# Attention and experts in one kernel: the main list turned four pauses later, weights split one call behind their load, the first expert product ordered behind the last attention sums

## The chip, the cores and the metric

The kernel runs on one core of one Trainium2 chip. A core has a matrix engine (TensorE, in the profile PE, with its weight loads as PEld), a vector engine (VectorE, DVE), an activation engine (ScalarE, ACT), a general engine (GpSimd, POOL), a queue engine that mostly issues transfers (SyncE, SP), and DMA engines that move data between memory and the core. Each engine takes its instructions in the order in which the program has them; semaphores make one wait for another. The metric is the device time of one execution in microseconds (us), lower is better. What can be told from no change in this study is about 0.3%.

## What is computed

The first half is linear attention for 8 batches, 8 heads, 576 tokens of 64 values, with features of exp(x) and exp(-x). The second half sends each of the 4608 tokens (512 values) through one of 8 experts, two products with a relu between them.

```python
def phi(x):
    proj = np.einsum('bhsd,df->bhsf', x, w_phi)
    proj = proj - np.max(np.abs(proj), axis=-1, keepdims=True)
    return np.concatenate([np.exp(proj), np.exp(-proj)], axis=-1)
q_p, k_p = (phi(q), phi(k))
kv = np.einsum('bhsf,bhsd->bhfd', k_p, v)
z = np.sum(k_p, axis=2)
num = np.einsum('bhsf,bhfd->bhsd', q_p, kv)
den = np.einsum('bhsf,bhf->bhs', q_p, z)[..., None] + 1e-06
x = num / den                      # to (B, S, 512)
...
fresh_e = int(np.argmax(logits[b, s]))
e = fresh_e if s == 0 or local_gate[b, s] < 0.5 else prev_e
...
h = np.maximum(x[b, s] @ w1[e], 0.0)
out[b, s] = p[e] * (h @ w2[e])
```

## The kernel before, in words

**Attention** runs in 72 steps over pairs of token chunks (`step`, L484). Its last sums are the matmuls of `num` (L404): they multiply the features of q with the summed kv, and DVE divides them (L421 to L424). In these steps the order on PE is the one in which the program is written; afterwards the planner orders PE too.

**The planner.** The program is written as tiles in pools and instructions that use them. A planner then reckons through the program and gives each engine its order: an instruction is issued when in its reckoning the inputs are there and a buffer of its pool is free, and the place in the code decides between instructions that are ready together. `issue_after(x)` puts what is written inside it behind instruction `x` on its engine; `high_priority` moves it up. A load or a split can therefore run far ahead of its place in the code.

**The experts** work on slots of up to four units of 128 tokens that share an expert. Two early slots (`eslots`, three units each) come from the first half of the batches and are worked while the list of all the rest is made; then come the slots of the main list (`moe`, L1196). The main list is planned by `plan_main` (L809): DVE counts, POOL gathers the list's rows into `lr` (L736), PE turns `lr` by two transposes (L753), DVE copies token numbers and probabilities (L755, L756). Then POOL can gather token rows `xg` (L984), and PE turns them (L1010).

**A slot** (`slots`, L1134) is `layer1` and `layer2`. `layer1` makes the hidden values in eight blocks of 128: a block is four groups of three matmuls (`three`, L1024 to L1026: high part by high part, low by high, high by low) into one of two PSUM banks (`psl`). Then ACT writes the relu's high part hh (L1063) and DVE the low part hl (L1064), after which the bank is free. For three units a block is 12 matmuls of 384 columns. `layer2` multiplies hh and hl with the second weights for each unit (again `three`), and DVE scales the result to y (L1122), which POOL scatters out (L1125).

**Pauses.** `layer1` calls a function from a list in the middle of each block and at its end, so a block has two pauses. For the two early slots these lists (`soon`, L158) hold the steps of planning: `go` and `rest` for the last gate in the first, `read` for the turn of the main list and `ahead` for its first gathers in the second. `read` is the next part of `plan_main`: L753 behind the last matmul written (`last_pe`), then L755 and L756. `later` holds the same for `layer2`: `listed` starts `plan_main` and its gathers.

**Weights.** A slot has eight slabs of 128 x 1024, four of each weight. `load` (L927) lets SP fetch a slab as `wraw` (512 KB, three buffers at this stage). `split` (L947) lets ACT cast it to a high part `whi` (L955) and DVE subtract to a low part `wlo` (L957). `spare` (L960) loads and splits one more slab if fewer are held than fit; `used` (L974) counts one slab as used and calls `spare`. `layer1` calls `used` after every second block, `layer2` calls `spare` or `used` after every second of its eight steps. The first early slot's slabs are loaded and split beside attention (`early_weights`, L472).

Of the kernel before, what the change touches and what calls it, by code (L numbers as in the profile page):

```python
# [55 lines left out]
class Kernel:  # L56
# [9 lines left out]
    def run(self):  # L66
        nc, tc, A = self.nc, self.tc, self.A
        act, dve = self.act, self.dve
        with ExitStack() as root:
            self.const = self.mkpool(root, "const", 1, "left")  # L70
            dram = self.mkpool(root, "dram", 1, "left", DRAM)
            self.xs = dram.tile([NT + 1, DM], F32, name="xs")


            self.lst = dram.tile([E * NT + 128, PLACE], F32, name="lst")
            first = self.const.tile([128, 256], F32, name="first")
            self.act.dma_start(first[:, 128:256], A["first"][:, 384:512])
            self.ident, self.w2 = first[:, 0:128], first[:, 128:256]
            self.cnt = self.const.tile([128, E], BF16, name="cnt")
            dve.memset(self.cnt, 0.0)  # L80

            warm = self.const.tile([128, E], BF16, name="warm")
            act.activation(warm, self.cnt, AF.Exp)

            self.wgi = self.const.tile([128, NHP, 2, 9], F32, name="wgi")
            self.pool.memset(self.wgi, 0.0)

            self.moe_early = self.mkpool(root, "moe_e", WE, "left")
            self.mxg = self.mkpool(root, "moe_xg", 2, "left")
            back, front = ExitStack(), ExitStack()  # L90
            self.back2 = self.mkpool(back, "back2", 2, "left")
            self.small = self.mkpool(back, "small", 1, "left")

            self.pr = self.small.tile([128, 2, NC, PLACE], F32, name="pr")
            self.pool.memset(self.pr, 0.0)
            self.pskv = self.mkpool(back, "pskv", 2, "left", PSUM)
            self.psb = self.mkpool(back, "psb", 2, "left", PSUM)


            self.front2 = self.mkpool(front, "front2", 2, "right")  # L100
            self.front3 = self.mkpool(front, "front3", 3, "right")
            self.feat = self.mkpool(front, "feat", 8, "right")
            self.psf = self.mkpool(front, "psf", 2, "right", PSUM)
            self.wphases = [(self.moe_early, WE)]

            self.scattering = False
            self.tail, self.eslots, self.scattered = False, [], []
            self.g, self.ch, self.kvb, self.lg, self.kvp, self.summed = {}, {}, {}, {}, {}, {}
            n = NBP * NHP * NC
            self.todo, self.turns, self.gates, self.background = [], [], [], []  # L110
            self.fetched = 0
            self.fetch_kq(0)
            self.fetch_kq(1)
            self.sp.dma_start(first[:, 0:128], A["first"][:, 256:384])
            self.fetch_v(0)
            self.fetch_v(1)
            self.fetch_kqv(2)
            self.consts()
            with tc.manual_schedule(engines={mybir.EngineType.PE}):
                for p in range(n // 2):  # L120
                    while self.fetched < n // 3 and self.fetched * 3 < 2 * p + 8:
                        self.fetch_kqv(self.fetched)
                    if p == FILL + 4:
                        self.background.append(self.table())
                    if FILL <= p < FILL + 4:
                        self.fill(p - FILL)
                    self.step(p, n)
            self.tail = True
            p = n // 2
            while p < n // 2 + KVLAG + 1 or self.todo or self.turns or self.gates:  # L130
                self.step(p, n)
                p += 1
            for x in self.background:
                for _ in x:
                    pass
            front.close()
            self.open_main(root)
            plan = self.plan_main()
            go = self.advance

            def rest():
                for _ in self.last_gate:
                    pass

            def listed():
                next(plan)
                next(plan)
                self.coming.append(self.by_size[4][0])

            def read():  # L150
                with tc.high_priority():
                    next(plan, None)
            no = lambda: None
            m = []

            def ahead():
                m.append(self.tokens(self.by_size[4][0], True))
            self.slots(self.eslots, soon=[[no, no, no, go, no, no, go, no, no, go, rest], [no, no, read, no, ahead]],  # L158
                       later=[[listed], [no, no] + [lambda k=k: m[0][k]() for k in range(4)]])
            back.close()  # L160
            self.open_rest(root)
            self.moe()
# [228 lines left out]
    def num(self, u, b, cs, kvs, bank=None):  # L391

        bp, hp = divmod(u, NHP)
        n, c0 = len(cs), cs[0]
        e = {}

        def mm(c, r, h, sg, kvs):
            i = u * NC + c
            q0 = i % 2 * 128
            if not e:  # L400
                t = bank or self.psb.tile([128, 512], F32, name="nm")
                e["t"] = t[:, 0:n * 2 * KV].rearrange("p (c k) -> p c k", c=n)
            k = slice(h * KV, h * KV + KV)
            self.pe.matmul(e["t"][r, c - c0, k], self.ch[i]["qp"][:, sg, h, q0 + r.start:q0 + r.stop],  # L404
                           kvs[:, sg, k], start=sg == 0, stop=sg == 1)


        for c in cs:
            k = [self.kvb[u] if c == 4 else kvs, kvs]
# [549 lines left out]

    def spare(self):  # L960

        while self.coming:
            s = self.coming[0]
            i = len(s.get("w", ()))
            if i == 8:
                self.coming.pop(0)
                continue
            if self.held < sum(n for _, n in self.wphases):
                self.load(s, i)
                self.split(s)  # L970
                self.held += 1
            return

    def used(self, n):  # L974
        for _ in range(n):
            self.held -= 1
            self.spare()
# [50 lines left out]
    def both(self, s, k, o, ah, al, c, first, last):  # L1028
# [6 lines left out]
        for z in (0, 1):  # L1035
            r = slice(64 * z, 64 * z + 64)
            self.last_pe = self.pe.matmul(o[r], ah.bitcast(F32)[:, r], w[z][:, c], start=first, stop=last)

    def hidden(self, n):
        return [self.mx2.tile([128, 8, n * 128], F32R, name=x, bufs=1) for x in ("hh", "hl")]  # L1040

    def layer1(self, s, between):

        act, dve = self.act, self.dve
        (xh, xl), w, n = s["x"], s["w"], s["n"]
        hh, hl = s["h"] = self.hidden(n)

        def pause():
            if between:
                between.pop(0)()  # L1050
        per = 2 if n == 2 else 1
        for f0 in range(0, 8, per):
            t = self.psl.tile([128, per, n * 128], F32, name="l1")
            for j in range(per):
                f = f0 + j
                wh, wl = w[f // 2]
                for d in range(4):
                    c = slice(d * 256 + f % 2 * 128, d * 256 + f % 2 * 128 + 128)
                    self.three(t[:, j, :], wh[:, c], wl[:, c], xh[:, d, :], xl[:, d, :], d == 0, d == 3)
                    if d % 2 and (d, j) != (3, per - 1):  # L1060
                        pause()
            hc = slice(f0, f0 + per)
            act.activation(hh[:, hc, :], t, AF.Relu)  # L1063
            dve.scalar_tensor_tensor(hl[:, hc, :], t, 0.0, hh[:, hc, :].bitcast(F32), ALU.max, ALU.subtract)  # L1064
            pause()
            if (f0 + per) % 2 == 0:
                self.used(1)
# [66 lines left out]
    def slots(self, order, held=None, soon=(), later=()):  # L1134
        first = order[0]
        if "x" not in first:
            for f in self.tokens(first):
                f()
        self.held = len(first.get("w", ()))
        self.coming = list(order)  # L1140
        for i, s in enumerate(order):
            while len(s.get("w", ())) < 8:
                self.spare()
            new = order[i + 1] if i + 1 < len(order) else None
            between = []
            for x in order[i + 1:i + 3 if new and len(new["ei"]) == 2 and s["n"] > 1 else i + 2]:
# [2 lines left out]
            if s["n"] > 1:  # L1149
                self.layer1(s, list(soon[i]) if i < len(soon) else [])  # L1150
                rest = between
            else:
                rest = self.layer1_one(s, between) + between
            if i < len(later):
                rest = list(later[i]) + rest
# [135 lines left out]
```

## Time and profile before

| | |
|---|---|
| times of three runs | 767.77, 768.43, 770.03 us (median 768.43) |
| the profiled execution | 768.59 us, of which the span is 766.8 us |
| attention's last sums (L404) | end near 299.6 us |
| first early slot, `layer1` and `layer2` | 299.5 to 337.7 us |
| second early slot, `layer1` begins | 337.74 us |
| the main list's gather issued by POOL (L736) | 336.87 to 338.37 us |
| main slabs 1, 2, 3, 4 issued by SP | 335.56, 337.64, 338.73, 341.98 us |

A timeline row has the start in us, the length in us, the engine, the line, the operation, the tile written and the tiles read, and in brackets the idle time in front of it and what ended it. A row of the waits has the waiting engine and line, what it waited for, the total in us, how many times, and the longest. A row of the windows has the stretch, its length, and busy time and count for PE, PEld, DVE, ACT and POOL, then the granted clock of PE, the share of DMA and GB/s. Matmuls overlap, so the step from one start to the next is what one costs, not its length.

### The profile page before, as it was taken

The numbers are of one execution on the slowest core, as the hardware profiler recorded it, in microseconds if no ns is written. First come the engines' busy times: TensorE is split into PE (matmuls) and PEld (weight loads), VectorE is DVE, ScalarE is ACT, GpSimd is POOL, SyncE is SP. The second block draws the span as 40 slices with busy tenths as digits, with TensorE's granted clock in tenths as the row PEclk, the third lists the DMA queues.
The fourth block names the chain that finished last, engine by engine and source line by source line (L and its number), as shares of the span: only waits on it lengthen the run. The fifth ranks groups of instructions, "written<-read, shape, count | busy, mean of one in ns | idle before, by whom it ended". The sixth has DMA issues, their size and how long they took to land. (4 is left out here: it accounts for less than half of the span.)

```text
span 766.8 us, 21974 instructions
## 1 busy us (share of the span) xinstructions
PE 739.7 (96%) x9319; PEld 637.3 (83%) x9319; DVE 451.0 (59%) x828; ACT 344.5 (45%) x648; POOL 181.9 (24%) x306
## 2 busy tenths in 40 slices
PE   7999999999998898989999999999999999999997
PEld 6999989989887887869888985789888768888885
DVE  5888888789878876665532347425323554544411
ACT  4776657666676664324421236314212453433300
POOL 0210103310374563433302041021202102101011
PEclk9999999999999999998999999999999999999999
DMA  6755545544766743248612799432398474432010
GB/s 201 240 169 140 152 127 141 152 130 138 227 179 182 217 118 107 86 149 275 205 52 69 287 366 324 146 124 82 124 352 284 142 242 165 138 123 97 1 38 29
DMA packets 66100, 125.04 MB, mean 163 GB/s; under 512 B 7220, under 2 KB 45300, under 8 KB 65950
## 3 DMA queue, kind: packets, MB, share of 16 engines
q1 hardware_dynamic: 57808, 101.03, 41.4%
q0 software_dynamic: 8016, 22.51, 8.2%
q8 instruction: 74, 1.21, 0.7%
q14 instruction: 26, 0.21, 0.1%
q10 hardware_dynamic: 176, 0.07, 0.0%
HBM read 102.05 MB, written 22.06 MB: 162 GB/s over the span
## 5 line engine op out<-in xcount | busy, mean ns | idle before, releaser
L955 ACT CAST whi<-wraw 128x1024 fp32r<-128x1024 f32 x88 | 92.2, 1048 | 134.5 <-PE l L1026 59.6
L957 DVE TENSOR_TENSOR wlo<-wraw,whi 128x1024 fp32r<-128x1024 f32 x80 | 97.8, 1223 | 88.7 <-ACT whi L955 88.6
L1024 PE MATMUL l<-xhi,whi 128*128 128x384 f32 (+2 forms) x352 | 127.1, 361 | 1.2 <-DVE g_es L617 0.6
L1026 PE MATMUL l<-xhi,wlo 128*128 128x384 f32 (+2 forms) x352 | 124.4, 353 | 0.0
L1025 PE MATMUL l<-xlo,whi 128*128 128x384 f32 (+2 forms) x352 | 124.3, 353 | 0.0
L1024 PE MATMUL l<-whi,hh 128*128 128x512 f32 x288 | 117.1, 407 | 0.0
L1025 PE MATMUL l<-wlo,hh 128*128 128x512 f32 x288 | 114.1, 396 | 0.0
L1026 PE MATMUL l<-whi,hl 128*128 128x512 f32 x288 | 113.6, 395 | 0.0
L285 ACT ACTIVATE kp<-sb 128x512 f32<-128x512 f32 x144 | 83.4, 625 | 58.5 <-DVE sb L281 55.5
L279 DVE TENSOR_REDUCE m<-pj 128x8 f32<-128x1024 f32 x72 | 87.7, 1218 | 35.0 <-PE pj L276 33.0
L1063 ACT ACTIVATE hh<-l 128x384 fp32r<-128x384 f32 (+1 forms) x84 | 44.9, 535 | 110.8 <-PE l L1026 110.8
L276 PE MATMUL pj<-first,kq 64*128 64x128 f32 x1152 | 85.8, 290 | 8.0 <-DMA kq<-in_kqT 4.2
L309 ACT ACTIVATE qp<-pj 128x512 f32<-128x512 f32 x144 | 79.6, 594 | 24.8 <-PE pj L294 12.9
L281 DVE TENSOR_TENSOR sb<-pj,m 128x1024 f32<-128x1024 f32 x72 | 88.1, 1223 | 3.5
L404 PE MATMUL nm<-kvs,qp 128*64 128x74 f32 x2304 | 88.4, 228 | 1.7 <-issue 0.9
L1064 DVE SCALAR_TENSOR_TENSOR hl<-l,hh 128x384 fp32r<-128x384 f32 (+1 forms) x84 | 51.4, 611 | 60.4 <-ACT hh L1063 60.3
L276 PEld LDWEIGHTS pj<-first,kq 64*128 64x128 f32 x1152 | 72.2, 192 | 15.1 <-issue 5.2
L404 PEld LDWEIGHTS nm<-kvs,qp 128*64 128x64 f32 x2304 | 80.6, 136 | 3.0 <-issue 1.5
L1024 PEld LDWEIGHTS l<-xhi,whi 128*128 128x128 f32 x352 | 66.8, 190 | 15.6 <-issue 5.6
L326 PE MATMUL kvp<-v,kp 128*64 128x65 f32 x2048 | 78.6, 226 | 1.0 <-issue 0.5
L1125 POOL DMA_INDIRECT out<-y,p_tokm x30 | 35.1, 1171 | 182.7 <-DVE y L1122 167.8
L326 PEld LDWEIGHTS kvp<-v,kp 128*64 128x64 f32 x2048 | 67.9, 139 | 5.6 <-ACT kp L285 1.2
(222 smaller groups left out, 926.1 us busy)
## 6 DMA issues: line engine op xcount, KB each, us to landing
wraw<-in_w1h SPq DMA_DIRECT2D x44, 512.0 KB
wraw<-in_w2h SPq DMA_DIRECT2D x44, 512.0 KB
kq<-in_kqT SPq DMA_DIRECT2D x47, 384.0 KB
v<-in_va SPq DMA_DIRECT2D x48, 195.0 KB
xs<-xo SPq DMA_DIRECT2D x48, 128.0 KB
whi<-in_w1h SPq DMA_DIRECT2D x8, 512.0 KB
wlo<-in_w1h SPq DMA_DIRECT2D x8, 512.0 KB
whi<-in_w2h SPq DMA_DIRECT2D x8, 512.0 KB
```

The source lines that it names most:

```text
L276: self.last_pe = self.pe.matmul(t[:, h, i % 2, j, :], kq[r, j, s], self.w2[r], start=True, stop=True)
L279: dve.tensor_reduce(m, f, AX.X, ALU.max, apply_absolute_value=True)
L281: self.last_dve = dve.tensor_sub(sb.rearrange("p h c j f -> p (h c j) f"), f, m.unsqueeze(2).broadcast_to([128, 8, 128]))
L285: self.last_act = act.activation(kp[:, :, :, sg, :].rearrange("p c h f -> p h c f"), sb[:, :, :, 0], AF.Exp, scale=1.0 - 2 * sg)
L309: self.act.activation(qp[:, sg].rearrange("p h (c r k) -> p (h c) r k", c=2, r=2), src, AF.Exp, scale=1.0 - 2 * sg)
L326: self.pe.matmul(t[r, sg, h], kp[:, h, sg, r], v[:, h], start=first and sg + h == 0, stop=last and sg + h == 2)
L404: self.pe.matmul(e["t"][r, c - c0, k], self.ch[i]["qp"][:, sg, h, q0 + r.start:q0 + r.stop], kvs[:, sg, k], start=sg == 0, stop=sg == 1)
L955: self.act.copy(hi, raw)
L957: (low or self.dve).tensor_sub(lo[:, c], raw[:, c], hi.bitcast(F32)[:, c])
L1024: mm(o, ah, bh, start=first, stop=False)
L1025: mm(o, ah, bl, start=False, stop=False)
L1026: self.last_pe = mm(o, al, bh, start=False, stop=last)
```

## The change

Three edits. `read` moves from the third entry of the second early slot's list to the seventh, and `ahead` from the fifth to the tenth. `spare` now first splits what the call before it loaded, then loads one slab and leaves its split to the next call; `asked` counts the loads of a slot in place of the finished splits, and a slot that begins splits whatever is still left. And the first matmuls of the first early slot's first product stand behind the last matmul of attention's sums on PE; `last_num` is used once and then empty.

```diff
-            self.slots(self.eslots, soon=[[no, no, no, go, no, no, go, no, no, go, rest], [no, no, read, no, ahead]],
+            self.slots(self.eslots, soon=[[no, no, no, go, no, no, go, no, no, go, rest], [no] * 6 + [read, no, no, ahead]],
...
-            self.pe.matmul(e["t"][r, c - c0, k], self.ch[i]["qp"][:, sg, h, q0 + r.start:q0 + r.stop],
+            self.last_num = self.pe.matmul(e["t"][r, c - c0, k], self.ch[i]["qp"][:, sg, h, q0 + r.start:q0 + r.stop],
...
     def spare(self):
+        self.landed()
         while self.coming:
             s = self.coming[0]
-            i = len(s.get("w", ()))
+            i = s.get("asked", len(s.get("w", ())))
             if i == 8:
                 self.coming.pop(0)
                 continue
             if self.held < sum(n for _, n in self.wphases):
                 self.load(s, i)
-                self.split(s)
+                s["asked"] = i + 1
+                self.loaded.append(s)
                 self.held += 1
             return
+
+    def landed(self, keep=0):
+        while len(self.loaded) > keep:
+            self.split(self.loaded.pop(0))
...
+    def behind(self):
+        x, self.last_num = self.last_num, None
+        return self.tc.issue_after(x.ins) if x else nullcontext()
...
-                    self.three(t[:, j, :], wh[:, c], wl[:, c], xh[:, d, :], xl[:, d, :], d == 0, d == 3)
+                    with self.behind():
+                        self.three(t[:, j, :], wh[:, c], wl[:, c], xh[:, d, :], xl[:, d, :], d == 0, d == 3)
...
-        self.held = len(first.get("w", ()))
-        self.coming = list(order)
+        self.held = first.get("asked", len(first.get("w", ())))
+        self.coming, self.loaded = list(order), getattr(self, "loaded", [])
         for i, s in enumerate(order):
-            while len(s.get("w", ())) < 8:
+            while s.get("asked", len(s.get("w", ()))) < 8:
                 self.spare()
+            self.landed()
```

## The prediction

> **What bounds the kernel now.** I read the page first, then the waits of TensorE, then the windows, then the timeline of each engine around the one wait that stands out.
>
> ```profile
> span 766.8 us, 21974 instructions
> PE 739.7 (96%) x9319; PEld 637.3 (83%) x9319; DVE 451.0 (59%) x828; ACT 344.5 (45%) x648; POOL 181.9 (24%) x306
> ```
>
> TensorE is busy for 96% of the span, so only its idle time and its clock can be won. Of its waits between 280 and 360 us, all at the seam from attention to the experts, one is large:
>
> ```profile
> PE pt L753 <- DMA lr<-lst,p_rim: 3.2, 1, 3.2
> PE l L1024 <- DVE g_es L617: 0.6, 1, 0.6
> PE l L1024 <- DVE hl L1064: 0.5, 1, 0.5
> ```
>
> The windows give PE, PEld, DVE, ACT, POOL, then the granted clock and the DMA. The clock falls to half late in 343.50:344.00 (0.92 is 16% of half a microsecond at half, so at 343.92) and is back at 350.75 (0.75: half of that stretch). After the seam PE is full: 400 to 420 stands for the later stages.
>
> ```profile
> 343.50:344.00 0.50, 0.00 (x0) 0.00 (x0) 0.00 (x0) 0.00 (x0) 0.40 (x1) 0.92 0.81 328
> 350.50:351.00 0.50, 0.50 (x3) 0.50 (x3) 0.00 (x0) 0.00 (x0) 0.50 (x1) 0.75 0.68 197
> 400.00:420.00 20.00, 20.00 (x94) 16.39 (x93) 4.96 (x7) 2.96 (x5) 4.91 (x5) 1.00 0.21 66
> ```
>
> So 3.2 us are idle and 6.8 us run at half clock: about 6.6 us at stake. The timeline of PE there:
>
> ```profile
> 337.74 0.33 PE L1024 MATMUL l<-xhi,whi 128*128 128x384 f32 x1
> ...
> 340.52 0.33 PE L1025 MATMUL l<-xlo,whi 128*128 128x384 f32 x1
> 340.69 0.34 PE L1026 MATMUL l<-xhi,wlo 128*128 128x384 f32 x1
> 344.23 0.42 PE L753 MATMUL pt<-first,lr 48*128 48x48 f32 x2 [3.20 <-DMA lr<-lst,p_rim]
> 344.58 0.69 PE L1024 MATMUL l<-xhi,whi 128*128 128x384 f32 x1
> ...
> 346.67 0.63 PE L1024 MATMUL l<-whi,hh 128*128 128x512 f32 x1
> 347.09 0.63 PE L1025 MATMUL l<-wlo,hh 128*128 128x512 f32 x1
> ...
> 348.37 0.52 PE L1024 MATMUL l<-xhi,whi 128*128 128x384 f32 x1
> ...
> 351.56 0.33 PE L1024 MATMUL l<-xhi,whi 128*128 128x384 f32 x1
> ```
>
> From 337.74 run block 0 of the second early slot (12 matmuls) and half of block 1 (6). Then the two transposes of the main list wait for their gather. Half a block, four matmuls of the second product and block 2 (348.37) follow; block 3 begins at 351.56. The question is whether block 2 really waited for L753. ACT and DVE answer:
>
> ```profile
> 339.64 1.05 ACT L955 CAST whi<-wraw 128x1024 fp32r<-128x1024 f32 x1 [3.44 <-DMA wraw<-in_w1h]
> 344.53 1.05 ACT L955 CAST whi<-wraw 128x1024 fp32r<-128x1024 f32 x1 [3.84 <-DMA wraw<-in_w1h]
> 345.49 0.48 ACT L1063 ACTIVATE hh<-l 128x384 fp32r<-128x384 f32 x1
> 345.87 1.04 ACT L955 CAST whi<-wraw 128x1024 fp32r<-128x1024 f32 x1
> ```
> ```profile
> 340.72 1.23 DVE L957 TENSOR_TENSOR wlo<-wraw,whi 128x1024 fp32r<-128x1024 f32 x1 [2.03 <-ACT whi L955]
> 341.87 0.74 DVE L1122 TENSOR_SCALAR y<-l,p_probe 128x512 f32<-128x512 f32 x1
> 345.61 1.23 DVE L957 TENSOR_TENSOR wlo<-wraw,whi 128x1024 fp32r<-128x1024 f32 x1 [3.00 <-ACT whi L955]
> 346.75 0.20 DVE L755 CAST p_tokm<-pt 128x48 int32<-128x48 f32 x1
> 346.87 0.20 DVE L756 COPY p_probm<-pt 128x48 f32<-128x48 f32 x1
> 346.99 0.55 DVE L1064 SCALAR_TENSOR_TENSOR hl<-l,hh 128x384 fp32r<-128x384 f32 x1
> ```
>
> Block 0 ended near 340.0, but its hh (L1063) stands on ACT behind the cast of the main list's second slab, which waits for its DMA until 344.53. There are two banks for the first product, so block 2 needs block 0's hl, done at 347.54. **Two waits lie side by side**, and removing the visible one uncovers the other.
>
> **The change part by part.** The sum is made against the profiled execution's own 768.59 us (span 766.8), 0.16 above the median of 768.43.
>
> **1. The main list four pauses on.** A block has two pauses, so `read` moves from the middle of block 1 to the middle of block 3, 24 matmuls later.
> - Block 1's other half follows at 0.173 a matmul (340.52 to 340.69) and ends at about 342.1. PE then waits for hh at 345.97: 3.9 idle in place of 3.2.
> - The four matmuls of the second product need only hh. At half clock they take 0.42 each (346.67 to 347.09), at full clock half of that. DVE's two copies go from in front of hl, which starts 0.24 earlier and ends at 347.30. Block 2 starts at 346.0 + 4 x 0.425 = 347.70 (cold) or 347.30 (warm), instead of 348.37: **-0.67 or -1.07**.
> - The transposes come back inside block 3 without a wait, 344.23 to 344.58: **+0.35**.
> - Clock: before, block 2 had 350.75 - 348.37 = 2.38 us at half clock, 1.19 lost. After, with the same instants, (350.75 - 347.70)/2 = 1.53: **+0.34**. If the clock falls one half of its 6.83 us later (347.33 to 354.17), block 2 starts warm: 3.43 - 1.19 = +2.24.
>
> Part 1 gives -0.67 + 0.35 + 0.34 = 0.0; with the late fall -1.07 + 0.35 + 2.24 = +1.5. A fall at 347.33 that ends at 350.75 gives -1.07 + 0.35 + 1.72 - 1.19 = -0.2.
>
> Behind the moved step stand two DVE copies and POOL's six gathers of token rows (before at 347.23 to 354.84). After, the copies run at about 352 and the gathers, 1.27 apart, are issued by about 361. Their first reader is at 367.81, so I cost this at nothing; were the rows later than that, each microsecond would be one of PE. SP's weight loads do not pass through `read`.
>
> ```profile
> 347.23 0.98 POOL L984 DMA_INDIRECT xg<-xs,p_tokm  x1 [3.33 <-DVE p_probm L756]
> 353.89 0.95 POOL L984 DMA_INDIRECT xg<-xs,p_tokm  x1 [0.30 <-PE l L1026]
> 367.81 0.60 PE L1010 MATMUL tr<-first,xg 128*128 128x128 f32 x4
> ```
>
> **2. Splits one call later.** Loads and splits keep their mutual order; only their place among the products moves. Does that move an instruction on ACT or DVE?
>
> ```profile
> 303.64 1.05 ACT L955 CAST whi<-wraw 128x1024 fp32r<-128x1024 f32 x1 [0.51 <-PE l L1025]
> 304.60 0.48 ACT L1063 ACTIVATE hh<-l 128x384 fp32r<-128x384 f32 x1
> ```
>
> This cast is written after block 5, yet runs ahead of block 1's hh: the planner issues what is ready, and the place in the code decides only between things ready together. The casts become ready by a freed buffer or a landed DMA. The new call also splits all that is left when a slot begins (`landed()` in `slots`), so the first three slabs of the main list are still written ahead of block 0's hh. **I take 0.** Bounds: the 1.1 of L1024's two short waits could go (-1.1); a slab late by one call costs up to 24 x 0.173 = 4.2, but slabs are ready long before use, as here by 24 us:
>
> ```profile
> 453.07 1.05 ACT L955 CAST whi<-wraw 128x1024 fp32r<-128x1024 f32 x1 [0.34 <-DMA wraw<-in_w1h]
> 477.27 0.50 PE L1024 MATMUL l<-xhi,whi 128*128 128x512 f32 x1
> ```
>
> **3. The first product behind the last sums.** One matmul now fills a hole:
>
> ```profile
> 295.06 0.44 PE L1024 MATMUL l<-xhi,whi 128*128 128x384 f32 x1
> 295.44 2.41 PEld L404 LDWEIGHTS nm<-kvs,qp 128*64 128x64 f32 x67 [0.19 <-ACT kvs L384]
> ```
>
> The sums wait 0.19 for ACT's copy of kvs, so without the matmul they would hardly start sooner. The matmul's 0.17 comes back behind them: **+0.17**, between -0.2 (they do start sooner) and +0.2. The products queue behind it; nothing but hh waits for them.
>
> Sum: 768.59 + 0.0 + 0 + 0.17 = **768.8**, with the other clock ends 768.5 to 770.3.
>
> **The rivals.**
> **A, the clock never falls.** PE is idle for 3.9 us, but with the four matmuls at full clock. Then -1.07 + 0.35 - 1.19 + 0.17 = -1.7: **766.9**. Against it: 3.2 idle were enough before. [...]
>
> **B, the order on ACT flips** (the planner puts block 0's hh ahead of the cast that waits). ACT is free at 340.69, hh ends at 341.1, DVE's y at 342.61, hl at 343.1: block 2 starts 5.27 earlier, no clock is lost: -5.27 - 1.19 + 0.35 + 0.17 = -5.9, **762.7**. If block 1's hh stays behind the cast, its hl ends at 347.3 and block 3 begins there instead of at 351.56: -4.26 + 0.35 + 0.17 = -3.7, **764.9**. For it: a landing half a microsecond later in the planner's reckoning is enough, and the splits have been lowered. Against it: nothing ahead of 341 that decides this order changes.
>
> **C, weights first (slower).** The third and fourth slabs, no longer held up, go ahead of block 0's hh and hl too. hh then comes at 347.6, hl after three more low parts (345.61 + 3 x 1.2 + 0.5) at 349.7: block 2 +1.33, transposes +0.35, part three +0.17, clock -0.66 or +1.05: **769.8 to 771.5**. It decides once hl ends after 348.37. For it: they are written ahead of hh. Against it: the third slab has that place already and still follows hh (345.87).
>
> **That part 2 reorders nothing** is my forecast, not a rival.
>
> **How the numbers follow.** Forecast 0.42 (768.5 to 770.3), A 0.12, B 0.30, C 0.16. The predicted time is 768.8. The range 762.5 to 770.6 takes in the forecast, A, B and C's lower part. About 0.3% (2.3 us) can be told from no change: faster is B and a little of A, 0.33; slower is C's upper half and the forecast's far end, 0.13; the same is 0.54.
>
> **What would show it.** Right: L753 without a wait, a wait of L1024 or of the second product's L1024 on ACT hh or DVE hl of 3 to 4 us from about 342, half clock behind it, ACT still cast, cast, hh. B: hh at about 340.6 and no gap over 2 us. C: two more casts before hh. I am wrong also if the second slab's DMA lands at another time than 344.5, or if PE has new idle after 360.

## The result, and the profile after

The changed kernel takes **771.69 us** (median of 20 runs) against 769.62 us for the kernel before (20 runs beside them): the ratio is **1.0027, interval 1.0015 to 1.0038**, so it is slower, by about 2.1 us, a size just under the 0.3% that can be told from no change in this study. One of the 20 executions ran at a mean granted clock of 0.655 and took 1016.62 us; the ratio is taken without it. The forecast was 768.8 us, "the same", and the time lies outside its range. The profiled execution took 771.9 us.

First two lines of the page, then the waits of TensorE between 280 and 370 us (the two largest), then the windows in which the clock changes:

```profile
span 770.1 us, 21970 instructions
PE 739.4 (96%) x9319; PEld 636.7 (83%) x9319; DVE 450.9 (59%) x828; ACT 344.4 (45%) x648; POOL 181.9 (24%) x306
```
```profile
PE l L1031 <- DVE hl L1077: 6.2, 2, 5.7
PE nm L404 <- issue: 1.0, 3, 0.4
```
```profile
347.00:347.50 0.50, 0.00 (x0) 0.00 (x0) 0.50 (x1) 0.50 (x2) 0.00 (x0) 0.53 0.49 197
353.50:354.00 0.50, 0.50 (x3) 0.50 (x3) 0.41 (x1) 0.00 (x0) 0.00 (x0) 0.64 0.84 344
```

The busy time is what it was (739.4 for 739.7); the span grew by idle time. The wait at the transposes is gone and a longer one, 5.7 us instead of 3.2, has come for hl (the new file's L1077 is L1064 of before, L1076 is L1063, L1031 to L1033 are L1024 to L1026; L753 and L955 keep their numbers). The half clock starts at 347.04 (0.53 is 94% of the half microsecond at half) and ends at 353.86: 6.83 us, as long as before, but 3.1 us later. Now TensorE's timeline around the gap, then ACT's:

```profile
342.53 0.34 PE L1033 MATMUL l<-xhi,wlo 128*128 128x384 f32 x1
348.59 0.69 PE L1031 MATMUL l<-xhi,whi 128*128 128x384 f32 x1 [5.71 <-DVE hl L1077]
...
354.31 0.42 PE L753 MATMUL pt<-first,lr 48*128 48x48 f32 x2
354.66 0.44 PE L1031 MATMUL l<-xhi,whi 128*128 128x384 f32 x1
...
357.89 0.40 PE L1031 MATMUL l<-whi,hh 128*128 128x512 f32 x1
358.13 0.39 PE L1032 MATMUL l<-wlo,hh 128*128 128x512 f32 x1
```
```profile
345.76 1.04 ACT L955 CAST whi<-wraw 128x1024 fp32r<-128x1024 f32 x1 [4.15 <-DMA wraw<-in_w1h]
346.71 0.48 ACT L1076 ACTIVATE hh<-l 128x384 fp32r<-128x384 f32 x1
```
```profile
346.84 1.23 DVE L957 TENSOR_TENSOR wlo<-wraw,whi 128x1024 fp32r<-128x1024 f32 x1 [3.31 <-ACT whi L955]
347.98 0.55 DVE L1077 SCALAR_TENSOR_TENSOR hl<-l,hh 128x384 fp32r<-128x384 f32 x1
```

The reader sees the chain that the prediction named: the second slab's DMA, its cast on ACT, hh behind it, hl on DVE, block 2. But block 2's first matmul (348.59) stands right at the end of the gap. The four matmuls of the second product, which ran ahead of block 2 before (346.67 to 348.37), come only from 357.89 on.

### The profile page after: what moved, and what is told of

Read it like the earlier page. It is cut to its first block, busy times and chain, and to the rows that moved or that the text cites. A ratio compares the mean times of both kernels' runs of the same rounds, so it can differ in the third digit from the quotient of the medians.

```text
span 770.1 us, 21970 instructions
## 1 busy us (share of the span) xinstructions
PE 739.4 (96%) x9319; PEld 636.7 (83%) x9319; DVE 450.9 (59%) x828; ACT 344.4 (45%) x648; POOL 181.9 (24%) x306
## 5 line engine op out<-in xcount | busy, mean ns | idle before, releaser
L955 ACT CAST whi<-wraw 128x1024 fp32r<-128x1024 f32 x88 | 92.1, 1048 | 136.9 <-PE l L1033 59.6
L1031 PE MATMUL l<-xhi,whi 128*128 128x384 f32 (+2 forms) x352 | 127.3, 362 | 6.8 <-DVE hl L1077 6.2
L1033 PE MATMUL l<-xhi,wlo 128*128 128x384 f32 (+2 forms) x352 | 124.7, 354 | 0.0
L1031 PE MATMUL l<-whi,hh 128*128 128x512 f32 x288 | 116.7, 405 | 0.0
L1033 PE MATMUL l<-whi,hl 128*128 128x512 f32 x288 | 113.9, 396 | 0.3 <-DVE hl L1077 0.3
L1076 ACT ACTIVATE hh<-l 128x384 fp32r<-128x384 f32 (+1 forms) x84 | 44.9, 535 | 111.4 <-PE l L1033 111.4
L404 PE MATMUL nm<-kvs,qp 128*64 128x74 f32 x2304 | 88.7, 228 | 2.7 <-issue 1.5
L1077 DVE SCALAR_TENSOR_TENSOR hl<-l,hh 128x384 fp32r<-128x384 f32 (+1 forms) x84 | 51.3, 611 | 61.1 <-ACT hh L1076 61.0
L1031 PEld LDWEIGHTS l<-xhi,whi 128*128 128x128 f32 x352 | 66.9, 190 | 21.4 <-DVE hl L1077 6.4
L404 PEld LDWEIGHTS nm<-kvs,qp 128*64 128x64 f32 x2304 | 80.4, 136 | 4.3 <-issue 2.6
```

The costliest lines, as they stand in the source:

```text
L404: self.last_num = self.pe.matmul(e["t"][r, c - c0, k], self.ch[i]["qp"][:, sg, h, q0 + r.start:q0 + r.stop], kvs[:, sg, k], start=sg == 0, ...
L955: self.act.copy(hi, raw)
L1031: mm(o, ah, bh, start=first, stop=False)
L1033: self.last_pe = mm(o, al, bh, start=False, stop=last)
```

## The experiments

Theory **W**, the wait handed on: what bounds the seam is block 0's hh behind the cast of the late second slab, and moving L753 out of the way only changes where TensorE stands still. Rivals: **G**, the gather's wait was a cost of its own; **S**, the third edit costs. And for the loss itself: **B**, the four matmuls are kept out of the gap by the bank of the transposes; **C**, only the gap's length and the clock count. All ratios are to the kernel before, timed beside them on the same chip. Four chips were used, and they turned out to differ where it matters (the kernel before takes 762.40 us on chip 10 and 768.59 on chips 2 and 7), so each part names its chip.

### The edits apart, a hold of the splits, and busy work in the gap (chip 10, before 762.40 us)

`p1_read_only` has the first edit alone; `p23_no_read` is the changed kernel without it:

```diff
-            self.slots(self.eslots, soon=[[no, no, no, go, no, no, go, no, no, go, rest], [no] * 6 + [read, no, no, ahead]],
+            self.slots(self.eslots, soon=[[no, no, no, go, no, no, go, no, no, go, rest], [no, no, read, no, ahead]],
```

> The kernel before with the first edit alone (the main list turned four pauses later). Theory W (the wait is handed on: block 2 of the second early slot waits for hl, which stands behind a cast that waits for its DMA, and the half clock behind it lasts longer): slower than before by 1.5 to 2.5 us, ratio 1.002 to 1.003; L753 without a wait, L1024 with one of 4 to 6 us on DVE hl. Rival S (the loss comes from the seam at attention's end, the third edit): ratio 1.000 within 0.001.

> The changed kernel with the main list turned where it was before, so the second and third edits alone. W: 0.0 to 0.2 us from before, ratio 1.000 within 0.001, L753 waits about 3.2 us again. S: ratio 1.002 to 1.003, with everything behind attention about 0.8 us late.

Measured: 1.0013 (0.9992 to 1.0034) and 1.0005 (0.9988 to 1.0022), neither to be told from no change. The first edit alone was expected to cost 1.002 to 1.003, with a wait of 4 to 6 us. The waits of TensorE between 280 and 380 show what is missing, first edit alone, then the other two:

```profile
PE l L1024 <- DVE hl L1064: 3.0, 3, 1.6
```
```profile
PE pt L753 <- DVE wlo L957: 1.3, 1, 1.3
PE l L1031 <- DVE hl L1077: 0.7, 1, 0.7
```

The wait changes its place as W has it, but on this chip either is 1.6 us at most, where 3.2 and more were expected, and the clock stayed at 1.00 there. There is little here to hand on.

`h3_weights_behind` takes hh out from behind the cast: in the changed kernel, the splits of the main list's first slabs are held behind hh and hl of block 3.

```diff
+                self.shut = self.by_size[4][0]
...
+            def open_():
+                self.shut = None
+                with tc.issue_after(self.last_hh.ins), tc.issue_after(self.last_hl.ins):
+                    self.landed()
...
-            self.slots(self.eslots, soon=[[no, no, no, go, no, no, go, no, no, go, rest], [no] * 6 + [read, no, no, ahead]],
+            self.slots(self.eslots, soon=[[no, no, no, go, no, no, go, no, no, go, rest], [no, no, no, no, no, no, read, open_, no, ahead]],
...
-        while len(self.loaded) > keep:
+        while len(self.loaded) > keep and self.loaded[0] is not getattr(self, "shut", None):
...
-            act.activation(hh[:, hc, :], t, AF.Relu)
-            dve.scalar_tensor_tensor(hl[:, hc, :], t, 0.0, hh[:, hc, :].bitcast(F32), ALU.max, ALU.subtract)
+            self.last_hh = act.activation(hh[:, hc, :], t, AF.Relu)
+            self.last_hl = dve.scalar_tensor_tensor(hl[:, hc, :], t, 0.0, hh[:, hc, :].bitcast(F32), ALU.max, ALU.subtract)
```

> The changed kernel, with the split of the main list's first three slabs held until the second early slot's block 3 has been evacuated: on ACT and DVE they stand behind hh and hl of block 3. W: the 5.7 us of idle and the 6.8 us at half clock go, the time is 4 to 7 us below before, ratio 0.991 to 0.995. Rival D (the DMA of the list and the slabs is what is late, and some other instruction waits for it): ratio 0.999 or more, with a new wait on PE of 2 us or more near there.

Measured: 0.9987 (0.9967 to 1.0007). TensorE has no wait of note left in the second early slot, and none over 0.7 us between 280 and 380, but the gain is about 1 us at most and not told from none. The size expected was missed. The likely reason is that the kernel before, which was not profiled on this chip, has as small a gap here as p23_no_read.

`spin_clock` was to keep the clock up by 32 added matmuls between blocks 1 and 2, which change no result.

```diff
+                with tc.issue_after(self.last_pe.ins):
+                    for _ in range(32):
+                        self.last_pe = self.pe.matmul(d, e["w"][0][0][:, 0:128], e["x"][0][:, 0, :], start=True, stop=True)
```

> The changed kernel with 32 matmuls more (384 columns, into a bank that nobody reads) between block 1 and block 2 of the second early slot: 5.5 us of work in place of the idle time, so PE is busy and its clock should stay full. If the half clock is a part of the loss: 2.5 to 3.4 us below the changed kernel, ratio to before 0.998 to 1.000, granted clock 1.00 from 340 to 360. If the loss is the idle time alone: as the changed kernel, ratio 1.002 to 1.003.

Measured: 1.0056 (1.0039 to 1.0072). The clock does not fall on this chip in the other three kernels either, so the run says nothing of it: the added work only costs time. The question of the clock stays open by this run.

### The second slab made late (chip 11, before 763.22 us)

To have the disputed wait whatever the chip, two copies of 512 KB from DRAM to DRAM go on SP's queue ahead of the second slab. The planner reckons with them and could put hh ahead of the cast by itself (rival B of the prediction), so late_slab_before and late_slab_after hold hh behind that cast, as it was. late_slab_free_hh has the hold of the splits from h3_weights_behind instead.

```diff
+        if i == 0 and hasattr(self, "by_size") and s is self.by_size[4][0]:
+            with self.tc.issue_after(x.ins):
+                for k in (0, 1):
+                    sp.dma_start(self.extra[k], self.A["w1h"][7, k])
...
+            if f0 == 0 and hasattr(self, "eslots") and s is self.eslots[1]:
+                with self.tc.issue_after(self.cast2.ins):
+                    act.activation(hh[:, hc, :], t, AF.Relu)
```

> The changed kernel once more, on the chip of the three runs below. Theory W (the wait is handed on: block 2 waits for block 0's hl, whose hh stands behind the cast of the late second slab): the result follows the slab. If the slab's cast waits 3.5 us or more for its DMA here, one idle stretch of 4 to 6 us ahead of block 2, half clock behind it, and a ratio of 1.002 to 1.004; if it waits under 2.6 us, an idle stretch under 2.5 us, no half clock, 1.000 to 1.002. Rival S (the product behind attention's sums costs): +0.5 us or more at the seam whatever the slab does, so 1.001 or more also where the slab is early.

> The kernel before, with two 512 KB copies from DRAM to DRAM put on SP's queue ahead of the main list's second slab, so that this slab lands some microseconds late, and block 0's hh held behind its cast, as in the kernel before. W: the gather's wait (L753) and the wait for hl grow together, PE is idle for 6 to 12 us near 340 to 355 and the clock falls behind that; ratio 1.006 to 1.014. If the slab were not what both waits hang on (rival G: the gather alone), idle stays under 3.5 us and the ratio under 1.003.

> The changed kernel with the same two copies and the same hold. W: L753 waits no more, and the whole idle time stands at block 2's first product, on hl: 0 to 3 us more than in late_slab_before, ratio 1.006 to 1.017. G (the gather was the bound, and taking it out of the way wins its wait): 3 us or more below late_slab_before.

> The same two copies, but the first splits of the main list are held behind the hh and hl of block 3, so that hh waits for no slab; no hold of hh behind the cast. W: no idle stretch over 1.5 us between 335 and 360 although the slab lands as late as in late_slab_after, no half clock there, ratio 0.997 to 1.003, that is 4 us or more below late_slab_after. Rival D (the late weights themselves cost, wherever hh stands): within 2 us of late_slab_after.

| run | us | ratio (interval) |
|---|---|---|
| after_again | 762.84 | 0.9991 (0.9971 to 1.0010) |
| late_slab_before | 766.60 | 1.0046 (1.0032 to 1.0061) |
| late_slab_after | 769.33 | 1.0075 (1.0053 to 1.0097) |
| late_slab_free_hh | 760.88 | 0.9966 (0.9949 to 0.9984) |

TensorE's rows at the end of the gap, for after_again, late_slab_before and late_slab_after:

```profile
342.08 0.44 PE L1031 MATMUL l<-xhi,whi 128*128 128x384 f32 x1 [3.23 <-DVE hl L1077]
```
```profile
345.43 0.43 PE L754 MATMUL pt<-first,lr 48*128 48x48 f32 x2 [5.00 <-DMA lr<-lst,p_rim]
...
349.15 0.63 PE L1032 MATMUL l<-wlo,hh 128*128 128x512 f32 x1
349.57 0.52 PE L1031 MATMUL l<-xhi,whi 128*128 128x384 f32 x1
```
```profile
347.11 0.69 PE L1038 MATMUL l<-xhi,whi 128*128 128x384 f32 x1 [6.15 <-DVE hl L1088]
```

The unaltered change costs nothing on this chip: its gap on hl is 3.23 us and the clock does not fall. What was expected from the cast's own wait was not met, though: ACT waits 4.34 us for the slab, about as in after (4.15), yet the gap is 2.5 us shorter, so that wait is not the measure.

```profile
339.25 1.04 ACT L955 CAST whi<-wraw 128x1024 fp32r<-128x1024 f32 x1 [4.34 <-DMA wraw<-in_w1h]
```

What counts here is how far the cast comes behind the products of block 0, and here it comes 2.0 us sooner behind them than on chip 7 (both are read in the last section), which is also the difference of the two gaps (3.23 and 5.27). With the slab made late the case comes back: 5.00 us at the transposes, with the second product's matmuls ahead of block 2 (349.57), become 6.15 us on hl without them, and the time rises by 2.73 us. G, which had it fall by 3, is out. Freeing hh of the late slab takes 8.45 us off late_slab_after, more than it lost to the kernel before, and a little more than expected (0.9966, expected 0.997 to 1.003); the late weights themselves cost nothing that shows, and the rival D is out. One expectation of W was too high: late_slab_before reached 1.0046, not 1.006, because the copies made the gap 5 us long and not 6 to 12.

### Which edit, and which bank (chip 2, before 768.59 us)

The same copies and hold with the first edit alone (`late_slab_read_only`), without it (`late_slab_no_read`), and with all three edits but the transposes of L753 in another bank (`late_slab_other_bank`). In the early slots those transposes and the second product take turns in two banks (`psb`, tag `nm`). `weights_behind_again` is h3_weights_behind on this chip, without copies.

```diff
-        t = self.pst([128, 2, n])
+        t = self.pskv.tile([128, 2, n], F32, name="pt", tag="kvp") if name == "m" else self.pst([128, 2, n])
```

> The first edit alone (the main list four pauses on), with the two copies and the hold of late_slab_before. W (the handed-on wait and what goes with it carry the loss): as late_slab_after, 1.0055 to 1.009, L753 without a wait, one stretch of 5 to 7 us on hl. Rival S (the third edit carries it): as late_slab_before, 1.003 to 1.005.

> The second and third edits without the first, with the copies and the hold. W: as late_slab_before, 1.003 to 1.0055, the wait at L753 and four matmuls of the second product ahead of block 2. S: 1.006 or more.

> late_slab_after with one thing changed: the transposes of L753 write to a bank of another pool, not to one of the two banks that the second product has. Theory B (with the first edit the transposes hold one of these two banks until block 3, so the four matmuls of the second product that ran ahead of block 2 cannot run there): they run in the gap again, the idle stretch is 0.7 to 1.1 us shorter than in late_slab_after, and the time 0.5 to 2 us lower, 1.004 to 1.0068. Rival C (the gap's length and the clock alone make the loss): 1.0065 to 1.0085, as late_slab_after.

> The kernel of h3_weights_behind once more, without copies: the changed kernel with the main list's first splits held behind hh and hl of block 3. W: nothing at the seam waits for a slab; below before by what the slab costs before on this chip: 0.997 to 0.999 where the second slab's cast waits 2 to 3 us there, 0.991 to 0.995 where it waits 3.5 us or more with half clock behind it. Rival N (no gain): 0.9995 or more.

| run | us | ratio (interval) |
|---|---|---|
| late_slab_read_only | 772.66 | 1.0061 (1.0041 to 1.0082) |
| late_slab_no_read | 769.49 | 1.0011 (1.0000 to 1.0021) |
| late_slab_other_bank | 771.15 | 1.0033 (1.0018 to 1.0047) |
| weights_behind_again | 763.20 | 0.9931 (0.9915 to 0.9948) |

The first edit alone carries the loss: with the copies, its kernel is 3.2 us above the one without it. S is out. (Without copies the edits were not run apart on a chip with a late slab.) late_slab_no_read came out below its range; a likely reading, not tested, is that on this chip the kernel before has a late slab already, so that the copies add little. TensorE at the end of the gap in late_slab_read_only, then in late_slab_other_bank:

```profile
347.90 0.69 PE L1031 MATMUL l<-xhi,whi 128*128 128x384 f32 x1 [6.92 <-DVE hl L1075]
```
```profile
348.43 0.79 PE L1038 MATMUL l<-whi,hh 128*128 128x512 f32 x1 [5.42 <-ACT hh L1085]
349.02 0.63 PE L1039 MATMUL l<-wlo,hh 128*128 128x512 f32 x1
349.45 0.63 PE L1038 MATMUL l<-whi,hh 128*128 128x512 f32 x1
349.88 0.63 PE L1039 MATMUL l<-wlo,hh 128*128 128x512 f32 x1
350.30 0.52 PE L1038 MATMUL l<-xhi,whi 128*128 128x384 f32 x1
```

With another bank for the transposes, the four matmuls stand in front of block 2 again, and TensorE waits for hh, not for hl. That is B's mechanism, shown: sharing the two banks kept them out. Why the bank that the transposes do not hold took none of them is not shown. The size is less sure. By the medians late_slab_other_bank is 1.5 us below late_slab_read_only, with intervals that overlap a little, and that kernel lacks the second and third edits; late_slab_after, which differs by the bank alone, ran on chip 11 only. The ratio of 1.0033 is also below the range expected (1.004 to 1.0068). Rival C had 1.0065 or more, but from the figures of chip 11, so this ratio alone does not close it. In its profile the half clock lasted 3.4 us, and 6.8 us in that of late_slab_read_only.

### Without copies, on a chip with a late slab (chip 7, before 768.59 us)

Last the question that stayed open: the bank without copies, and whether the hold of the splits makes the gain alone. `weights_behind_third` is h3_weights_behind on this chip, and `behind_early_read` is the same with `read` back in block 1; on TensorE the two differ only by the place of the two transposes.

```diff
-            self.slots(self.eslots, soon=[[no, no, no, go, no, no, go, no, no, go, rest], [no, no, no, no, no, no, read, open_, no, ahead]],
+            self.slots(self.eslots, soon=[[no, no, no, go, no, no, go, no, no, go, rest], [no, no, read, no, no, no, no, open_, no, ahead]],
```

> The changed kernel once more, for comparison with the next three on one chip. Handed-on wait (W): where the second slab's cast waits 3.5 us or more, 4 to 6 us idle ahead of block 2 on hl and 1.001 to 1.004; where it waits less, under 3.5 us idle and 0.998 to 1.002.

> The changed kernel with the transposes of L753 in a bank of another pool, without copies. Theory B (the bank that the transposes hold keeps the second product out of the gap): three of its matmuls run ahead of block 2 and fill 0.5 to 1.3 us of the gap; 0.5 to 1.5 us below after_third where the slab is late, within 1 us of it where it is early. Rival C (length and clock alone): within 0.4 us of after_third on a late slab too.

> The kernel of weights_behind_again with the transposes back in the middle of block 1: hh is free of the slab, but L753 waits for its gather again. Theory W2 (both waits must go together; each alone leaves the other): 2 to 4 us idle at L753 and, where the clock falls, up to 3.4 us of loss behind it; 2 to 6 us above weights_behind_third on a late slab, about 1 us above it on an early one. Rival H (the hold of the splits is the whole gain, and the place of the transposes does not count): within 1 us of weights_behind_third.

> The kernel of h3_weights_behind on the chip of the three above: no idle stretch over 1 us at the seam, no half clock there; 0.991 to 0.9955 on a late slab, 0.997 to 0.999 on an early one.

| run | splits held | L753 | us | ratio (interval) |
|---|---|---|---|---|
| before | no | block 1 | 768.59 | 1 |
| after_third | no | block 3 | 771.24 | 1.0029 (1.0018 to 1.0040) |
| other_bank | no | block 3, other bank | 770.00 | 1.0022 (1.0010 to 1.0034) |
| behind_early_read | yes | block 1 | 767.33 | 0.9982 (0.9968 to 0.9996) |
| weights_behind_third | yes | block 3 | 763.15 | **0.9932 (0.9912 to 0.9952)** |

One window of 15 us, from 340 to 355, tells the four changed kernels apart (the stretch, its length, busy time of PE, PEld, DVE, ACT, POOL, the granted clock, DMA): after_third, other_bank, behind_early_read, weights_behind_third.

```profile
340.00:355.00 15.00, 9.73 (x41) 9.11 (x40) 7.19 (x10) 5.09 (x7) 1.16 (x2) 0.77 0.78 247
```
```profile
340.00:355.00 15.00, 11.39 (x50) 10.25 (x49) 7.19 (x10) 6.00 (x9) 2.35 (x3) 0.77 0.73 243
```
```profile
340.00:355.00 15.00, 11.45 (x57) 11.10 (x56) 3.01 (x8) 3.14 (x6) 6.75 (x7) 0.89 0.71 214
```
```profile
340.00:355.00 15.00, 15.00 (x84) 14.31 (x84) 7.45 (x12) 6.25 (x9) 7.57 (x7) 1.00 0.74 233
```

The change as it is leaves 5.27 us idle. Its half clock lasts 6.8 us, to 353.59; the part of it that meets work begins with block 2 at 348.08, so it loses (353.59 - 348.08)/2 = 2.8 us. With both waits gone TensorE is full at full clock. The sum, 8.0 us, is close to the 8.1 us between the two medians. TensorE at the end of the gap, in after_third and in other_bank:

```profile
348.08 0.69 PE L1031 MATMUL l<-xhi,whi 128*128 128x384 f32 x1 [5.27 <-DVE hl L1077]
```
```profile
345.93 0.79 PE L1031 MATMUL l<-whi,hh 128*128 128x512 f32 x1 [3.61 <-ACT hh L1076]
346.52 0.63 PE L1032 MATMUL l<-wlo,hh 128*128 128x512 f32 x1
346.95 0.63 PE L1031 MATMUL l<-whi,hh 128*128 128x512 f32 x1
```

Without copies too, the other bank lets matmuls of the second product, three of them, into the gap. It saves 1.2 us by the medians, half of that by the ratios, whose intervals overlap: its mechanism is shown, its size is not settled beyond 0.5 to 1.2 us.

In behind_early_read hh is free, and the gather's wait is there again:

```profile
PE pt L759 <- DMA lr<-lst,p_rim: 3.6, 1, 3.6
```

So each wait stands ready behind the other: the change alone costs 2.65 us, the hold with `read` at its old place saves 1.3, both together save 5.4. On this chip the wait at the transposes counts as soon as hh is free: behind_early_read is 4.2 us above weights_behind_third, and rival H is out. In its profile the wait is 3.55 us and the half clock behind it, 3.41 us with work throughout, loses 1.7 us; these 5.3 us are more than the medians give. In weights_behind_third ACT shows the order that does it, four hh with no cast between, and three casts behind them:

```profile
339.50 0.49 ACT L1082 ACTIVATE hh<-l 128x384 fp32r<-128x384 f32 x1 [3.82 <-DVE y L1141]
341.58 0.49 ACT L1082 ACTIVATE hh<-l 128x384 fp32r<-128x384 f32 x1 [1.59 <-PE l L1039]
343.66 0.49 ACT L1082 ACTIVATE hh<-l 128x384 fp32r<-128x384 f32 x1 [1.59 <-PE l L1039]
346.30 0.49 ACT L1082 ACTIVATE hh<-l 128x384 fp32r<-128x384 f32 x1 [2.15 <-PE l L1039]
346.69 2.94 ACT L961 CAST whi<-wraw 128x1024 fp32r<-128x1024 f32 x3
```

This kernel is 8.1 us below the changed one on chip 7. Against the kernel before it is at 0.9931 and 0.9932 on chips 2 and 7, and at 0.9987 on chip 10, where the interval reaches 1.0007.

## Why the prediction was wrong, step by step

- **Two waits side by side, and the second uncovered by the removal of the first: right.** L753 waits no more, the same engine waits for hl instead, and ACT's order (cast, cast, hh) is the one forecast. late_slab_before against late_slab_after repeats it, and the last table shows it from both sides.
- **"The four matmuls of the second product need only hh", and fill the end of the gap: this step failed.** It reckoned with their inputs and not with the place that they write to. The transposes share two banks with the second product; written later, they hold one until DVE has copied it out (the copies start at 354.77 and 354.89), and the planner put none of the four ahead of block 2. PE was therefore idle for 5.7 us instead of the 3.9 reckoned. Block 2 did start earlier, as reckoned (348.59 - 338.55 = 10.04 us behind the slot's first product instead of 348.37 - 337.74 = 10.63: -0.59, forecast -0.67 to -1.07; the slab's cast came 0.42 us later behind that product than before, 7.21 for 6.79). But the four were still to do: 4 x 0.235 = **+0.94** (two steps from 357.89 to 358.36). The runs with the other bank show that the shared banks are the cause.
- **The clock: it fell, for 6.83 us as before, and the size taken was too small.** I took the fall at the same instant as before (+0.34) and kept the late fall (+2.24) as the far end. What came lies between the two: low until 353.86, so (353.86 - 348.59)/2 - 1.19 = **+1.45**. Block 2 began about where it was reckoned; the low stretch did not stay where it was. Its end moved from 13.0 to 15.3 us behind the slot's first product. Why by so much the runs do not show. The late fall, one half of 6.83 us on, was an estimate of mine that no run shows; measured, the clock fell 3.1 us later (at 347.04 instead of 343.92).
- **L753 back inside block 3, +0.35: right** (354.31 to 354.66). **The token gathers hidden: right**; no wait on them is among those of TensorE.
- **The second edit at nothing and the third at +0.17: not contradicted.** Together they measured 1.0005 (0.9988 to 1.0022), and with the late slab 1.0011 (1.0000 to 1.0021), and in either 0.17 us would pass unseen.
- **The sum.** -0.59 + 0.94 + 0.35 + 1.45 + 0.17 = +2.3, against the +2.07 of the medians; the 0.17 is the forecast's own, too small for these runs to measure. The rest of the distance to the forecast is its base: the kernel before took 768.59 us in the profiled execution, and 769.62 in the runs beside the changed kernel. The two profiled spans differ by more, 3.3 us, but 0.8 of that is there in attention already (sums of L404 start at 291.20 and 292.00 us), ahead of the places that the edits change.
- **The rivals.** A needed a clock that never falls: so it was without copies on chips 10 and 11, where the gaps are smaller too (3.23 us in after_again, single waits of 1.6 us at most on chip 10); not here. B (hh ahead of the waiting cast) did not happen, but it was the right thing to want: made by hand, with the casts held back and `read` in block 3, it gives 5.4 us on chips 2 and 7, about its 5.9. C's two further casts did not come ahead of hh: the third stands behind it at 347.10.

## What to carry to other kernels

Before a wait is removed, follow every other chain that ends at the same place: here a DMA held a cast, the cast held an activation behind it in ACT's queue, and that held TensorE (in after, ACT stood 4.15 us for the slab and TensorE 5.71 us for hl); the gather's DMA held it beside that (3.20 us in before). On chip 7 the change, which moves the transposes only out of the gather's way, lost 0.3%, freeing hh alone won 0.2%, and both won 0.7%; on chip 10, where the slabs come earlier, both won 0.1%, not told from nothing. Work that is to fill a gap needs its output buffer as well as its inputs; here moving one user of two banks kept four matmuls out of a gap of 5.7 us, and with another bank for it three came back (other_bank). A cast that waits for a DMA should not be queued ahead of work that TensorE needs next: with the late slab, freeing hh of it took 8.45 us off.

## What the runs showed of the hardware

**The half clock lasted 6.8 or 3.4 us, at no fixed distance from the idle time.** Summed over the windows between 340 and 356 us, it lasted 6.80 to 6.84 us in eight profiles (before, after, after_third, other_bank, late_slab_before, late_slab_after, late_slab_read_only and late_slab_no_read), 3.40 and 3.41 us in two (late_slab_other_bank, behind_early_read), and in the other eight the granted clock is 1.00 there. It began 2.1 us after the idle time did in other_bank, 2.9 in before, 4.2 in after, and in behind_early_read only at 347.45, when TensorE had been at work again for 1.5 us:

```profile
347.00:347.50 0.50, 0.50 (x5) 0.50 (x4) 0.00 (x0) 0.00 (x0) 0.50 (x1) 0.95 0.12 49
350.50:351.00 0.50, 0.50 (x3) 0.50 (x3) 0.00 (x0) 0.00 (x0) 0.35 (x1) 0.64 0.77 303
```

And 3.23 us idle in after_again brought no fall where 3.20 us in before did. What sets the start and the length the runs do not show.

**The chips differed in when the slabs came.** On chips 10 and 11 the kernel before takes 762.4 and 763.2 us, on 2 and 7 it takes 768.6. In after_again (chip 11) the cast of the second slab starts at 339.25, 4.7 us behind the slot's first product at 334.52; in after_third (chip 7) at 345.25, 6.8 us behind its first product at 338.48. SP issued the first slab 4.42 and 2.61 us ahead of that product. In p1_read_only (chip 10), late_slab_after and late_slab_free_hh (chip 11) it was 4.36 to 4.42 us ahead too, in before 2.18 and in after 1.82. DVE makes the expert numbers that these loads need (L712) 3.47 us ahead of that product in before and 3.78 in after. So the difference is there when SP issues the loads, ahead of any transfer of a slab. Why they are issued earlier on two chips is not shown. The same change measures 0.9991 on chip 11 and 1.0029 on chip 7, and with both waits gone the three chips measured are within 2 us of each other (761.4 to 763.2). That the slabs make this difference is likely, not shown apart: the kernel before was not profiled on these chips.
